# Attention and a greedy mixture of experts on one core: threshold searches in eight four-bit digits, and row lists from halves of 32 and 12 values

## The chip, the cores and the metric

The kernel runs on one core of one Trainium2 chip. A core has five engines that run their own instruction streams side by side: TensorE (PE, matrix products; its weight loads are listed apart as PEld), VectorE (DVE), ScalarE (ACT), GpSimd (POOL) and SyncE (SP, which issues most transfers here). They wait for one another by semaphores. The metric is the time of one execution on the device in microseconds, as the median of several runs; less is better.

## What is computed

First attention within clusters, then a layer of experts in which tokens are dealt out greedily by the size of their logits:

```python
N, D, E, F = (3072, 512, 8, 1024)
cap = N // E
logits = x @ w_gate            # x is the output of the attention
order = np.argsort(-logits.flatten())
for idx in order:
    tok, e = (int(idx) // E, int(idx) % E)
    if assigned[tok] >= 0 or counts[e] >= cap:
        continue
    assigned[tok] = e
    counts[e] += 1
...
for e in range(E):
    mask = assigned == e
    h = np.maximum(x[mask] @ w1[e], 0.0)
    out[mask] = h @ w2[e]
```

So each of the 8 experts gets exactly 384 of the 3072 tokens.

## The kernel before

Attention takes the first 370 us or so of the execution; the change touches none of its steps. The expert stage that follows treats the experts one after another, in the order in which they fill up. The code counts them p = 0 to 7; "the first expert" is p = 0, and "expert 2" means p = 2. For every expert there is

- a search for the logit at which it is full, digit by digit from the top. For each digit, `ind` (DVE) marks for 24 tokens a partition and each of the digit's values which tokens lie above it; `cnt` (PE, line 1212) counts the marks per expert; `blk0` and `blk1` (DVE) gather the counts; `pick` (PE, line 1240) spreads them over the partitions; `sat` (DVE) compares with 384; `dig` (PE, line 1253) turns the result into the threshold so far, which the next `ind` reads. After the upper digits `v` (DVE) forms the rest, and the next `ind` marks that.
- a row list of 384 token numbers. `top` and a few DVE steps (c1, c2, c3, ei, mq, gt, ge) name the expert; `rank` (PE, lines 1304 and 1305) ranks its members; `upe`, `scan`, `addr`, `stt0`, `pm`, `ph`, `pl` (DVE) turn ranks into a row number in two halves; `ohl` and `ohh` (DVE, lines 1341 and 1350) are one-hot marks of the low and of the high half; `ohv` (line 1344) is ohl times the token's number; `col` (PE, line 1357) multiplies ohv by ohh; `pb0`, `pb1` (DVE), `rep` (PE), `pi` and `idx` (DVE) put the list in place. Small tables of both stages lie in PSUM (`pk`, `pc`).
- `gx`, a gather of the 384 rows of x through the list (POOL's queue), and `xp` with `xc`, or `xt`, which bring them into place as `xgt`.
- eight weight loads (`w_load`, SP's queue), each issued once `reg` knows the expert's number, and their split in a high and a low 16-bit part: `wsc` and `whi` on ACT, `wlo` on POOL.
- `hid` (PE, line 1447): 8 blocks of 12 matmuls with 384 columns; after each block `rel` (ACT, writes hh) and `hlo` (DVE, line 1479, writes the rest hl). The products lie in five PSUM buffers `pf`.
- `out` (PE, line 1485): 72 matmuls with 512 columns, `oev` (ACT), and `sc`, the scatter to the output.

The order of the steps on each engine is fixed: a table written out in the source, `FFN_ORDER`, names the steps one after another, and each engine runs its own in that order. The search for expert p begins among the out matmuls of expert p-2 and ends, with the row list, among the hid matmuls of expert p-1. A step such as `cnt,3,1` is the count of digit 1 of expert 3; `hid,2,4,1,0` is a matmul of expert 2's block 4; `hlo,2,4` is the hl step of that block.

A search before has seven digits, of 5, 5, 5, 5, 4, 4 and 4 bits, 32 bits in all. For a 32-value digit `ind` works on 128x768, and the count is six matmuls of 32 columns; for a 16-value digit it is 128x384 and three matmuls of 64 columns. A row number of 0 to 383 is split in a low half of 16 and a high half of 24 values.

Of the kernel before, what the change touches and what calls it, by code (L numbers as in the profile page):

```python
# [191 lines left out]
w_load,0,1 stt0,0 pm,0 w_load,0,2 ph,0 pl,0 w_load,0,3 ohl,0 ohvp,0 ohh,0 lt,0 upd,0 col,0 wm,36 b,1,0 wm,37 wm,38 pb0,0
pb1,0 b,1,5 rep,0 wm,39 wm,40 b,1,6 wm,41 pi,0 wm,42 wm,43 idx,0 whi,0,0,B wm,44 wm,45 b,1,8 wm,46 gx,0,0 wm,47 b,1,1
wm,48 wm,49 wm,50 b,1,2 wm,51 wm,52 wm,53 wsc,0,1 wm,54 b,1,3 wm,55 wm,56 gx,0,1 b,1,4 b,1,9 whi,0,1,C gx,0,2 b,1,10
cnt,1,0,- wlo,0,0,B blk0,1,0 blk1,1,0 xph,0 xph,1 pick,1,0 xch,0 sat,1,0 xch,1 wsc,0,2 whi,0,2,C wsc,0,3 hid0,0,0,0,0
hid0,0,0,0,1 dig,1,0 ind,1,1,- hid0,0,4,0,0 hid0,0,4,0,1 wlo,0,1,C ei2 hid0,0,0,0,2 hid0,0,1,0,0 reg2 hid0,0,1,0,1
# [5 lines left out]
hid0,0,0,2,1 hid0,0,4,1,2 cnt,1,2,- hid0,0,5,1,0 hid0,0,5,1,1 hid0,0,5,1,2 hid0,0,6,1,0 blk0,1,2 hid0,0,6,1,1
hid0,0,6,1,2 hid0,0,7,1,0 hid0,0,7,1,1 blk1,1,2 hid0,0,7,1,2 hid0,0,4,2,0 hid0,0,4,2,1 hid0,1,0,0,0 wlo,0,3,C pick,1,2
hid0,0,0,2,2 hid0,0,1,2,0 hid0,0,1,2,1 sat,1,2 hid0,0,1,2,2 hid0,0,2,2,0 hid0,0,2,2,1 hid0,0,2,2,2 hid0,0,3,2,0 dig,1,2
hid0,0,3,2,1 hid0,0,3,2,2 hid0,0,0,3,0 hid0,0,0,3,1 v,1 hid0,0,4,2,2 hid0,0,5,2,0 hid0,0,5,2,1 hid0,0,5,2,2 ind,1,3,-
hid0,0,6,2,0 hid0,0,6,2,1 hid0,0,6,2,2 hid0,0,7,2,0 hid0,0,7,2,1 wsc,0,4 hid0,0,7,2,2 hid0,0,4,3,0 hid0,0,4,3,1
hid0,1,0,0,1 hid0,1,4,0,0 hid0,1,4,0,1 hid0,1,0,0,2 hid0,1,1,0,0 hid0,1,1,0,1 hid0,1,1,0,2 hid0,1,2,0,0 hid0,1,2,0,1
cnt,1,3,- hid0,0,0,3,2 hid0,0,1,3,0 hid0,0,1,3,1 whi,0,4,C hid0,0,1,3,2 blk0,1,3 hid0,0,2,3,0 hid0,0,2,3,1 hid0,0,2,3,2
hid0,0,3,3,0 blk1,1,3 hid0,0,3,3,1 hid0,0,3,3,2 hid0,0,4,3,2 hid0,0,5,3,0 pick,1,3 hid0,0,5,3,1 hid0,0,5,3,2
hid0,0,6,3,0 hid0,0,6,3,1 sat,1,3 hid0,0,6,3,2 hid0,0,7,3,0 hid0,0,7,3,1 wsc,0,5 hid0,0,7,3,2 wlo,0,4,C dig,1,3  # L210
hid0,1,2,0,2 hid0,1,3,0,0 hid0,1,3,0,1 hid0,1,3,0,2 ind,1,4,- hid0,1,0,1,0 hid0,1,0,1,1 hid0,1,4,0,2 hid0,1,5,0,0
hid0,1,5,0,1 hid0,1,5,0,2 hid0,1,6,0,0 hid0,1,6,0,1 hid0,1,6,0,2 cnt,1,4,- whi,0,5,C hid0,1,7,0,0 hid0,1,7,0,1
hid0,1,7,0,2 hid0,1,4,1,0 blk0,1,4 hid0,1,4,1,1 hid0,1,0,1,2 hid0,1,1,1,0 hid0,1,1,1,1 hid0,1,1,1,2 blk1,1,4
hid0,1,2,1,0 hid0,1,2,1,1 hid0,1,2,1,2 hid0,1,3,1,0 pick,1,4 hid0,1,3,1,1 hid0,1,3,1,2 wsc,0,6 hid0,1,0,2,0 hid0,1,0,2,1
wlo,0,5,C sat,1,4 hid0,1,4,1,2 hid0,1,5,1,0 hid0,1,5,1,1 hid0,1,5,1,2 dig,1,4 hid0,1,6,1,0 hid0,1,6,1,1 hid0,1,6,1,2
hid0,1,7,1,0 ind,1,5,- hid0,1,7,1,1 hid0,1,7,1,2 hid0,1,4,2,0 hid0,1,4,2,1 hid0,1,0,2,2 hid0,1,1,2,0 rel0,0,0
# [5 lines left out]
hid0,1,5,3,1 hid0,1,5,3,2 hid0,1,6,3,0 hid0,1,6,3,1 ind,1,6,- hid0,2,4,0,0 hid0,2,4,0,1 hid0,1,6,3,2 hid0,1,7,3,0
hid0,1,7,3,1 hid0,1,7,3,2 hid0,2,0,0,2 hid0,2,1,0,0 whi,0,7,C cnt,1,6,- hid0,2,1,0,1 hid0,2,1,0,2 hid0,2,2,0,0
hid0,2,2,0,1 blk0,1,6 hid0,2,2,0,2 hid0,2,3,0,0 hid0,2,3,0,1 hid0,2,3,0,2 hid0,2,0,1,0 blk1,1,6 hid0,2,0,1,1
hid0,2,4,0,2 hid0,2,5,0,0 hid0,2,5,0,1 pick,1,6 rel0,1,0 hid0,2,5,0,2 hid0,2,6,0,0 wlo,0,7,C hid0,2,6,0,1 hid0,2,6,0,2
sat,1,6 hid0,2,7,0,0 hid0,2,7,0,1 hid0,2,7,0,2 hid0,2,4,1,0 dig,1,6 rel0,1,1 top,1 hid0,2,4,1,1 hlo0,1,0,D hid0,2,0,1,2
# [10 lines left out]
lt,1 col,1 w_load,1,6 upd,1 hid0,2,7,3,2 out,0,0,3,0 pb0,1 rel0,2,1 out,0,0,3,1 w_load,1,7 out,0,0,3,2 pb1,1 out,0,0,4,0
out,0,0,4,1 wsc,1,0 b,2,0 rep,1 out,0,0,4,2 pi,1 out,0,0,5,0 idx,1 out,0,0,5,1 b,2,5 out,0,0,5,2 gx,1,0 b,2,6 whi,1,0,C
out,0,0,6,0 b,2,8 out,0,0,6,1 out,0,0,6,2 b,2,9 out,0,0,7,0 out,0,0,7,1 wsc,1,1 gx,1,1 out,0,0,7,2 out,0,1,0,0 b,2,1
out,0,1,0,1 out,0,1,0,2 b,2,2 out,0,1,1,0 whi,1,1,C out,0,1,1,1 b,2,3 gx,1,2 out,0,1,1,2 out,0,1,2,0 b,2,4 out,0,1,2,1  # L240
hlo0,1,1,D cnt,2,0,- wsc,1,2 out,0,1,2,2 wlo,1,0,C out,0,1,3,0 b,2,10 out,0,1,3,1 blk0,2,0 out,0,1,3,2 blk1,2,0
# [1297 lines left out]
```

## Time and profile before

| what | value |
|---|---|
| median of 3 runs (lowest to highest) | 676.03 us (675.4 to 678.72) |
| the profiled execution, its own time | 675.39 us |
| its span, from the first to the last instruction | 673.6 us |
| PE busy, share of the span | 644.6 us, 96% |
| DVE busy | 505.7 us, 75% |
| ACT busy | 418.9 us, 62% |
| POOL busy | 484.4 us, 72% |

The span is what the trace shows; the time of the execution is 1.8 us longer. Busy time is the sum of an engine's instructions without the gaps, and it mixes stages with different limits. Matmuls are pipelined: the duration of one in a row is longer than the distance to the next, and it is the distance that counts. A row of the trace in order of time has the start, the duration, the engine, the line, the operation, the tiles (out<-in), the shapes, and in brackets the idle time ahead of it with what ended it, where there was any.

### The profile page before, as it was taken

To read this page: it belongs to the slowest core of one execution; us is meant where nothing else is said; L and a number is where in the kernel's file an instruction comes from. 1 tells how busy PE (TensorE), PEld (TensorE's weight loads), DVE (VectorE), ACT (ScalarE), POOL (GpSimd) and SP (SyncE) were. 2 spreads that over 40 slices of the span, in tenths; PEclk is the share of its full clock that TensorE was granted. 3 is DMA by queue.
4 is the path that set the end of the run, shared out by engine and by line. 5 is a ranking of instruction groups with operands and counts; after the bars stand their busy time and mean duration, and the time that the engine had idled before them with its cause. 6 is when DMAs were issued, how large, how long until landed. Compare 5 with 4: busy or idle time off the path is not lost. (4 is left out here: it accounts for less than half of the span.)

```text
span 673.6 us, 19685 instructions
## 1 busy us (share of the span) xinstructions
PE 644.6 (96%) x8246; PEld 433.5 (64%) x8246; DVE 505.7 (75%) x1160; ACT 418.9 (62%) x552; POOL 484.4 (72%) x390
## 2 busy tenths in 40 slices
...
GB/s 191 197 205 167 163 153 231 114 179 164 169 197 132 168 178 139 98 142 55 52 50 74 26 175 130 307 92 300 150 241 208 183 251 157 264 322 164 48 1 47
DMA packets 175450, 105.84 MB, mean 157 GB/s; under 512 B 135426, under 2 KB 160002, under 8 KB 175362
## 3 DMA queue, kind: packets, MB, share of 16 engines
...
## 5 line engine op out<-in xcount | busy, mean ns | idle before, releaser
L838 POOL TENSOR_TENSOR rt<-pt 128x768 f16<-128x768 f32 x176 | 266.9, 1542 | 62.4 <-ACT pt L830 62.2
L830 ACT ACTIVATE pt<-sc 128x768 f32<-128x768 f32 x192 | 150.5, 811 | 102.3 <-PE sc L827 99.5
L788 DVE TENSOR_REDUCE mxs<-sc 128x1 f32<-128x768 f32 x192 | 178.7, 951 | 12.6 <-PE sc L784 11.2
L1447 PE MATMUL pf<-xgt,w1h 128*128 128x384 f16 (+1 forms) x640 | 129.6, 295 | 0.3 <-DVE xgt L1436 0.3
L860 PE MATMUL av<-vh,pt 128*128 128x66 f16 x1152 | 121.7, 194 | 0.2 <-DVE xb L893 0.2
L841 PE MATMUL av<-vh,rt 128*128 128x66 f16 x1152 | 121.4, 193 | 0.0
L862 PE MATMUL av<-vl,pt 128*128 128x64 f16 x1152 | 121.4, 191 | 0.0
L860 PEld LDWEIGHTS <-pt 128*128 128x128 bf16 x1152 | 106.0, 97 | 8.3
L862 PEld LDWEIGHTS <-pt 128*128 128x128 bf16 x1152 | 105.5, 98 | 8.7 <-issue 0.7
L841 PEld LDWEIGHTS <-rt 128*128 128x128 f16 x1152 | 104.7, 97 | 0.0
L823 PE MATMUL sc<-qbt,kbt 99*128 99x384 f16 x384 | 93.8, 325 | 1.0 <-DMA qbt<-mt 0.4
L827 PE MATMUL sc<-qat,kat 128*128 128x384 f16 x384 | 93.7, 325 | 0.0
L784 PE MATMUL sc<-kbt,qbt 80*128 80x384 f16 x384 | 90.2, 325 | 1.5 <-ACT qbt L746 0.7
L1447 PE MATMUL pf<-xgt,w1l 128*128 128x384 f16 (+1 forms) x320 | 90.5, 295 | 0.0
L1447 PEld LDWEIGHTS <-w1h 128*128 128x128 f16 x640 | 57.8, 98 | 28.5 <-issue 1.0
L1411 POOL TENSOR_TENSOR w2l<-wr,w2h 128x1024 f16<-128x1024 f32 x32 | 67.6, 2134 | 4.2 <-ACT w2h L1404 3.9
L1485 PE MATMUL pf<-w2h,hh 128*128 128x512 f16 x184 | 69.6, 378 | 0.0
L1485 PE MATMUL pf<-w2h,hl 128*128 128x512 f16 x184 | 69.4, 378 | 0.0
L1485 PE MATMUL pf<-w2l,hh 128*128 128x512 f16 x184 | 69.4, 378 | 0.0
L1401 ACT ACTIVATE wr<-wr 128x1024 f32<-128x1024 f32 x63 | 65.7, 1046 | 4.3 <-DMA wr<-in_moe_w_dram 3.6
L1411 POOL TENSOR_TENSOR w1l<-wr,w1h 128x1024 f16<-128x1024 f32 x31 | 65.4, 2136 | 0.3
L1479 DVE SCALAR_TENSOR_TENSOR hl<-pf,hh 128x384 f16<-128x384 f32 x56 | 30.7, 551 | 40.7 <-ACT hh L1476 36.6
(259 smaller groups left out, 1137.1 us busy)
## 6 DMA issues: line engine op xcount, KB each, us to landing
...
xg<-xrow,idx POOLq DMA_INDIRECT x24, 6.5
```

The costliest lines, as they stand in the source:

```text
L784: nc.tensor.matmul(p[:, half, :S // 2], QBT[u][:D + C, i, :], KBT[u][:D + C, h * J + half * 3:h * J + half * 3 + 3, :], start=True, stop=True)
L788: nc.vector.tensor_reduce(mxs[u % 3][:, i:i + 1], MP.pop((u, i))[:, :, :S // 2], axis=AX.XY, op=OP.max)
L823: nc.tensor.matmul(ps[:, half, :S // 2], KBT[u][:ER + 3, s, :], QBT[u][:ER + 3, cs, :], start=True, stop=False)
L827: nc.tensor.matmul(ps[:, half, :S // 2], KAT[u][:, s, :], QAT[u][:, cs, :], start=False, stop=True)
L830: nc.scalar.activation(pts[(u * 12 + s // 2) % RP][:, s % 2], MP.pop((u, "b", s))[:, :, :S // 2], AF.Exp, scale=ESC)
L838: (nc.vector if e == "D" else nc.gpsimd).tensor_sub(rts[x][:, s % 2], p.rearrange("p a b -> p (a b)"), hi_view(pts[x])[:, s % 2])
L841: nc.tensor.matmul(o[:, j, :], r[:, j * P:(j + 1) * P], VH[u][:, s, :], start=False, stop=(s % J == J - 1), skip_group_check=True)
L860: nc.tensor.matmul(o[:, j, :], hi[:, js], VH[u][:, s, :], start=(kt == 0 and j == 0), stop=False, skip_group_check=True)
L862: nc.tensor.matmul(o[:, j, :D], hi[:, js], VL[u][:, s, :], start=False, stop=False, skip_group_check=True)
L1411: nc.gpsimd.tensor_sub(lo, wrs[c], hi)
L1447: nc.tensor.matmul(o, (w1l if i == 2 else w1h)[x][:, c, fs], xgt[x][:, h + int(i == 1), ts], start=(first and i == 0), stop=(last and i == ...
L1485: nc.tensor.matmul(PS["o", p, g], (hl if i == 2 else hh)[x][:, f, g * P:(g + 1) * P], (w2l if i == 1 else w2h)[x][:, f, :], start=(f == 0 ...
```

## The change

From p = 2 on a search has eight digits of four bits: every `ind` is 128x384 and every count three matmuls of 64 columns. The tables for it (`offs4`, and `wdb4`, one for the upper and one for the lower four digits) are made on POOL with steps `tab4` and `wdb4`, put in behind `wdb` in the search of the first expert and behind the last `wlo` of that expert. `clr` clears the accumulators at the start of a search. From p = 1 on the row list takes a low half of 32 and a high half of 12 values: `ohl` and `ohv` go from 128x384 to 128x768, `ohh` from 128x576 to 128x288, `col` from three matmuls of 192 columns to six of 48, and `pb0`, `pb1`, `rep` and `pi` shrink.

```diff
+    SH4 = [28, 24, 20, 16, 12, 8, 4, 0]
+    offs4 = [rt.tile([P, 16], F32, name=f"offs4{r}") for r in range(4)] + [o[:, :16] for o in offs[3:]]
+    wdb4 = [rt.tile([P, P], BF16, name=f"wdb4{r}") for r in range(2)]
...
+    def lw(p):
+        return 32 if p else 16
...
+    def four(p):
+        return p >= 2
+
+    def digits(p):
+        return [16] * 8 if four(p) else DIG
...
     def f_cnt(p, r, h):
-        n, ind, oh = DIG[r], marks(p, r), ohs[w3(p)]
+        n, ind, oh = digits(p)[r], marks(p, r), ohs[w3(p)]
...
+    def f_wdb4(x):
+        nc.gpsimd.memset(wdb4[x], 0.0)
+        for i in range(4):
+            nc.gpsimd.memset(wdb4[x][32 * i:32 * i + 16, :], float(1 << SH4[4 * x + i]))
+            nc.gpsimd.memset(wdb4[x][32 * i:32 * i + 1, :], LEAST if i + x == 0 else 0.0)
+
+    def f_clr(p):
+        V.memset(satb, 0.0)
...
     def f_ohl(p):
-        V.tensor_tensor(ohl, plo[:, :, None].to_broadcast([P, NT, 16]), loc[:, None, :].to_broadcast([P, NT, 16]), op=OP.is_equal)
+        w = lw(p)
+        V.tensor_tensor(lo_of(ohl_, p), plo[:, :, None].to_broadcast([P, NT, w]),
+                        (loc32 if p else loc)[:, None, :].to_broadcast([P, NT, w]), op=OP.is_equal)
...
     def f_col(p):
-        k = GC[16]
-        PS["i"] = pq = pct.tile([P, k, CAP // 16], F32, name="pc")
+        k, w = GC[lw(p)], CAP // lw(p)
+        PS["i"] = pq = pct.tile([P, k, w], F32, name="pc")
         for i in range(0, NT, k):
-            nc.tensor.matmul(pq, ohv[:, i:i + k, :].rearrange("p t n -> p (t n)"), ohh[:, i:i + k, :],
+            nc.tensor.matmul(pq, lo_of(ohv_, p)[:, i:i + k, :].rearrange("p t n -> p (t n)"), hi_of(p)[:, i:i + k, :],
                              start=(i == 0), stop=(i + k == NT))
```

`FFN_ORDER` is written anew from the first count of expert 2 on; one line of it shows how:

```diff
-out,0,1,4,0 whi,1,2,C hlo0,2,0,D pick,2,0 out,0,1,4,1 out,0,1,4,2 out,0,1,5,0 sat,2,0 out,0,1,5,1 hlo0,2,1,D wsc,1,3
+out,0,1,3,0 b,2,10 out,0,1,3,1 out,0,1,3,2 pick,2,0 out,0,1,4,0 sat,2,0 whi,1,2,C hlo0,2,0,D out,0,1,4,1 out,0,1,4,2
```

Counted in PE work, the searches of experts 3 to 6 end 1.9, 2.7, 3.2 and 3.6 us later against the matmuls of the expert at hand, and the row lists, the first weight loads and the gathers of those experts with them. wsc, whi and wlo keep their places among the matmuls.

The first place is the row list of expert 5 on DVE. In the order before, the steps from upe (line 1328) to pb0 (line 1361) stand so; L1341 is ohl, L1350 ohh, L1344 ohv, L1325 lt and L1479 an hl step of expert 4:

```order
L1328 SCALAR_TENSOR_TENSOR L_98<-pk_8055,L_98 128x192
L1308 SCALAR_TENSOR_TENSOR tot_8083<-pc_10462,mk_8081 128x48
L1311 TENSOR_TENSOR pk_8055<-tot_8083,pc_10462 128x48
L1315 SCALAR_TENSOR_TENSOR pk_8055<-pk_8055,mk_8081 128x48
L1318 TENSOR_REDUCE pk_8055<-pk_8055 128x24
L1335 TENSOR_SCALAR pk_8055<-pk_8055 128x24
L1338 TENSOR_SCALAR pk_8055<-pk_8055 128x24
L1341 TENSOR_TENSOR ohl_8084<-pk_8055,loc_171 128x384
L1350 TENSOR_TENSOR ohh_8086<-pk_8055,hic_172 128x576
L1344 TENSOR_TENSOR ohv_8085<-ohl_8084,pk_8055 128x384
L1325 TENSOR_SCALAR pk_8055<-pk_8055 128x24
L1479 SCALAR_TENSOR_TENSOR hl0_8120<-pf_10404,hh0_8118 128x384
```

In the changed order the same stretch reads so; the line numbers are those of the changed source, in which L1546 is hl, L1402 ohl, L1413 ohh and L1406 ohv, and the fence begins with the first hl step behind upe:

```order
L1546 SCALAR_TENSOR_TENSOR hl0_8128<-pf_10437,hh0_8126 128x384
L1368 SCALAR_TENSOR_TENSOR tot_8091<-pc_10534,mk_8089 128x48
L1371 TENSOR_TENSOR pk_8055<-tot_8091,pc_10534 128x48
L1375 SCALAR_TENSOR_TENSOR pk_8055<-pk_8055,mk_8089 128x48
L1378 TENSOR_REDUCE pk_8055<-pk_8055 128x24
L1395 TENSOR_SCALAR pk_8055<-pk_8055 128x24
L1398 TENSOR_SCALAR pk_8055<-pk_8055 128x24
L1402 TENSOR_TENSOR ohl_8092<-pk_8055,loc32_8083 128x768
L1546 SCALAR_TENSOR_TENSOR hl0_8128<-pf_10461,hh0_8126 128x384
L1413 TENSOR_TENSOR ohh_8094<-pk_8055,hic32_8084 128x288
L1546 SCALAR_TENSOR_TENSOR hl0_8128<-pf_10487,hh0_8126 128x384
L1406 TENSOR_TENSOR ohv_8093<-ohl_8092,pk_8055 128x768
```

Three hl steps stand between upe and ohv where there was none; on PE, 22 hid matmuls lie between rank and col in both orders.

The second place is PE in the round of expert 3 in which v is formed. Before, between the dig (line 1253) and the first of the six matmuls of the next count (line 1212), there are seven out matmuls (the rows of the weight loads ahead of each matmul are left out here and in the next piece):

```order
L1253 MATMUL pc_9554<-satb_8067,wdb2_8071 128x1
L1485 MATMUL pf_9541<-w2h1_8109,hl1_8121 128x512
L1485 MATMUL pf_9541<-w2h1_8109,hh1_8119 128x512
L1485 MATMUL pf_9541<-w2l1_8111,hh1_8119 128x512
L1485 MATMUL pf_9541<-w2h1_8109,hl1_8121 128x512
L1485 MATMUL pf_9541<-w2h1_8109,hh1_8119 128x512
L1485 MATMUL pf_9541<-w2l1_8111,hh1_8119 128x512
L1485 MATMUL pf_9541<-w2h1_8109,hl1_8121 128x512
L1212 MATMUL pc_9568<-oh2_8059,ind1_8061 128x32
```

After (dig is line 1313, out line 1552, the count line 1249):

```order
L1313 MATMUL pc_9605<-satb_8067,wdb40_8081 128x1
L1552 MATMUL pf_9579<-w2h1_8117,hl1_8129 128x512
L1552 MATMUL pf_9579<-w2h1_8117,hh1_8127 128x512
L1552 MATMUL pf_9579<-w2l1_8119,hh1_8127 128x512
L1552 MATMUL pf_9579<-w2h1_8117,hl1_8129 128x512
L1249 MATMUL pc_9614<-oh2_8059,ind1_8061 128x64
```

Four out matmuls are left between the two, and the `ind` between them on DVE has 128x384 in place of 128x768.

The third place is DVE in expert 3's first round. Before, the hl steps (line 1479) of expert 1 stand around blk0 (1217), blk1 (1220), sat (1246) and ind (1193) so:

```order
L1479 SCALAR_TENSOR_TENSOR hl1_8121<-pf_9329,hh1_8119 128x384
L1217 TENSOR_TENSOR cq_8062<-pc_9458,own32_179 128x32
L1220 TENSOR_REDUCE cs_8063<-cq_8062 128x8
L1479 SCALAR_TENSOR_TENSOR hl1_8121<-pf_9365,hh1_8119 128x384
L1246 TENSOR_SCALAR scr0_8064,satb_8067<-pc_9475 32x8
L1479 SCALAR_TENSOR_TENSOR hl1_8121<-pf_9388,hh1_8119 128x384
L1193 SCALAR_TENSOR_TENSOR ind1_8061<-pk_8055,pc_9483,offs1_156 128x768
```

After, with hl at line 1546, clr at 1295, sat at 1305 and ind at 1230:

```order
L1546 SCALAR_TENSOR_TENSOR hl1_8129<-pf_9365,hh1_8127 128x384
L1295 MEMSET satb_8067 128x1
L1255 TENSOR_TENSOR cq_8062<-pc_9501,own16_177 128x64
L1258 TENSOR_REDUCE cs_8063<-cq_8062 128x8
L1546 SCALAR_TENSOR_TENSOR hl1_8129<-pf_9401,hh1_8127 128x384
L1305 TENSOR_SCALAR scr0_8064,satb_8067<-pc_9510 16x8
L1230 SCALAR_TENSOR_TENSOR ind1_8061<-pk_8055,pc_9518,offs41_8078 128x384
L1546 SCALAR_TENSOR_TENSOR hl1_8129<-pf_9424,hh1_8127 128x384
```

The last hl step of expert 1, which the third out matmul behind dig reads, now stands behind ind, and before it stood ahead of it.

## Rows read from the trace of the kernel before

**Rows 1.** Busy time by stretch: span, then us, busy (instructions) of each engine, clock, DMA.

```profile
core 0 of [0], span 673.6 us
...
500.00:550.00 50.00, 50.00 (x342) 26.62 (x341) 35.23 (x124) 28.93 (x39) 33.26 (x21) 1.00 0.57 177
```

**Rows 2.** PE in order of time, search of expert 3: counts, digs and neighbours.

```profile
491.32 0.30 PE L1212 MATMUL pc<-oh,ind 128*128 128x32 bf16 x6
491.48 0.38 PE L1485 MATMUL pf<-w2h,hh 128*128 128x512 f16 x1
...
499.46 0.17 PE L1253 MATMUL pc<-satb,wdb 128*128 128x1 bf16 x1
...
501.00 0.32 PE L1212 MATMUL pc<-oh,ind 128*128 128x32 bf16 x6
...
503.62 0.26 PE L1212 MATMUL pc<-oh,ind 128*128 128x64 bf16 x3
503.71 0.38 PE L1485 MATMUL pf<-w2h,hl 128*128 128x512 f16 x1
...
505.25 0.17 PE L1253 MATMUL pc<-satb,wdb 128*128 128x1 bf16 x1
...
506.16 0.26 PE L1212 MATMUL pc<-oh,ind 128*128 128x64 bf16 x3
```

**Rows 3.** PE in order of time: rank and col of expert 2, col of expert 5.

```profile
450.78 0.19 PE L1304 MATMUL pc<-mk,tri 128*128 128x48 bf16 x1
...
454.40 0.41 PE L1357 MATMUL pc<-ohh,ohv 128*128 128x192 f16 x3
454.65 0.49 PE L1447 MATMUL pf<-xgt,w1h 128*128 128x384 f16 x2
...
547.37 0.41 PE L1357 MATMUL pc<-ohh,ohv 128*128 128x192 f16 x3
```

**Rows 4.** DVE in order of time: ohv of experts 2 and 5.

```profile
453.67 0.54 DVE L1344 TENSOR_TENSOR ohv<-ohl,pk 128x384 f16<-128x384 f16 x1
...
546.72 0.54 DVE L1344 TENSOR_TENSOR ohv<-ohl,pk 128x384 f16<-128x384 f16 x1
```

**Rows 5.** DVE by form, 400 to 640: count, busy us, mean ns, idle before.

```profile
L1193 DVE SCALAR_TENSOR_TENSOR ind<-pk,pc,offs 128x384 bf16<-128x384 f32 x18 | 11.2, 622 | 6.9 <-PE pc L1253 6.9
...
L1350 DVE TENSOR_TENSOR ohh<-pk,hic 128x576 f16<-128x576 int32 x7 | 5.2, 747 | 0.0
...
L1341 DVE TENSOR_TENSOR ohl<-pk,loc 128x384 f16<-128x384 int32 x7 | 3.9, 557 | 0.2
```

**Rows 6.** DVE in order of time: an hl step of expert 2, v of expert 3.

```profile
485.49 0.54 DVE L1479 SCALAR_TENSOR_TENSOR hl<-pf,hh 128x384 f16<-128x384 f32 x1
485.96 0.17 DVE L1371 SCALAR_TENSOR_TENSOR pg<-pc,own 128x24 f32<-128x24 f32 x1
...
499.70 0.26 DVE L1197 SCALAR_TENSOR_TENSOR pk<-pk,pc,lop 128x24 f32<-128x24 int32 x1 [0.50 <-issue]
499.99 0.96 DVE L1191 TENSOR_TENSOR ind<-pk,offs 128x768 bf16<-128x768 f32 x1
```

**Rows 7.** PE in order of time: searches of expert 2 (two rows) and expert 3.

```profile
437.35 0.38 PE L1485 MATMUL pf<-w2h,hl 128*128 128x512 f16 x1
437.75 0.16 PE L1253 MATMUL pc<-satb,wdb 128*128 128x1 bf16 x1
...
473.35 0.17 PE L1240 MATMUL pc<-cs,rep 128*128 128x8 f16 x1 [0.40 <-DVE cs L1220]
```

**Rows 8.** DVE in order of time: copies into xgt in expert 2's search.

```profile
436.20 1.29 DVE L748 COPY xgt<-pf 128x1024 f16<-128x1024 f16 x2 [0.45 <-PE pc L1240]
```

**Rows 9.** POOL in order of time: the first expert's search and list.

```profile
391.78 0.83 POOL L1347 TENSOR_TENSOR ohv<-ohl,vals 128x384 f16<-128x384 f16 x1 [6.58 <-DVE ohl L1341]
```

**Rows 10.** SP's queue in order of time: first weight loads of expert 6.

```profile
576.53 2.12 SPq L1387 DMA_DIRECT2D wr<-in_moe_w_dram  x4
```

**Rows 11.** ACT in order of time: expert 6's first wsc.

```profile
580.21 1.06 ACT L1401 ACTIVATE wr<-wr 128x1024 f32<-128x1024 f32 x1 [0.71 <-DMA wr<-in_moe_w_dram]
```

More of the change, by code (lines that the diff above doesn't have):

```diff
@@ L192 @@
[L192 to L196, printed above, removed]
@@ L202 @@
[L202 to L206, printed above, removed]
@@ L207 @@
[L207 to L216, printed above, removed]
@@ L222 @@
[L222 to L226, printed above, removed]
@@ L237 @@
[L237 to L241, printed above, removed]
@@ L257 @@
[L257 to L259 removed]
+sat,0,1 wdb,5 dig,0,1 ind,0,2,0 ind,0,2,1 cnt,0,2,0 wdb,6 cnt,0,2,1 sat,0,2 dig,0,2 wdb,7 tab4,0 tab4,1 tab4,2 tab4,3
+tab4,4 tab4,5 wdb4,0 v,0 ind,0,3,0 ind,0,3,1 cnt,0,3,0 cnt,0,3,1 sat,0,3 dig,0,3 ind,0,4,0 ind,0,4,1 cnt,0,4,0 cnt,0,4,1
@@ new lines @@
+sat,0,4 dig,0,4 ind,0,5,0 ind,0,5,1 cnt,0,5,0 cnt,0,5,1 sat,0,5 dig,0,5 ind,0,6,0 ind,0,6,1 cnt,0,6,0 cnt,0,6,1 sat,0,6
+dig,0,6 top,0 c1,0 c2,0 c3,0 ei,0 mq,0 reg,0 gt,0 ge,0 es2,0 rank,0 wm,0 upe,0 wm,29 wm,30 w_load,0,0 wm,31 scan,0 wm,32
+wm,33 wm,34 addr,0 wm,35 w_load,0,1 stt0,0 pm,0 w_load,0,2 ph,0 pl,0 w_load,0,3 ohl,0 ohvp,0 ohh,0 lt,0 upd,0 col,0
+wm,36 b,1,0 wm,37 wm,38 pb0,0 pb1,0 b,1,5 rep,0 wm,39 wm,40 b,1,6 wm,41 pi,0 wm,42 wm,43 idx,0 whi,0,0,B wm,44 wm,45
+b,1,8 wm,46 gx,0,0 wm,47 b,1,1 wm,48 wm,49 wm,50 b,1,2 wm,51 wm,52 wm,53 wsc,0,1 wm,54 b,1,3 wm,55 wm,56 gx,0,1 b,1,4
@@ L281 @@
-blk1,3,6 hid,2,2,0,0 wlo,2,7,C hid,2,2,0,1 rel,2,1 pick,3,6 hid,2,2,0,2 hid,2,2,1,0 sat,3,6 hid,2,2,1,1 hlo,2,1 dig,3,6
-top,3 hid,2,2,1,2 hid,2,2,2,0 hid,2,2,2,1 c1,3 hid,2,2,2,2 c2,3 hid,2,2,3,0 hid,2,2,3,1 c3,3 hid,2,2,3,2 ei,3
-hid,2,3,0,0 mq,3 reg,3 hid,2,3,0,1 rel,2,2 hid,2,3,0,2 gt,3 hid,2,3,1,0 ge,3 hid,2,3,1,1 es2,3 rank,3 hid,2,3,1,2 upe,3
-hid,2,3,2,0 w_load,3,0 hid,2,3,2,1 scan,3 hid,2,3,2,2 hid,2,3,3,0 addr,3 hid,2,3,3,1 w_load,3,1 hid,2,3,3,2 stt0,3
-hid,2,4,0,0 pm,3 hid,2,4,0,1 rel,2,3 w_load,3,2 hid,2,4,0,2 ph,3 hid,2,4,1,0 pl,3 hid,2,4,1,1 ohl,3 hid,2,4,1,2
@@ L306 @@
-wlo,3,7,C hid,3,0,1,0 sat,4,5 hid,3,0,1,1 dig,4,5 hid,3,0,1,2 hid,3,0,2,0 ind,4,6,- hid,3,0,2,1 hid,3,0,2,2 hid,3,0,3,0
-cnt,4,6,- hid,3,0,3,1 hid,3,0,3,2 blk0,4,6 hid,3,1,0,0 blk1,4,6 hid,3,1,0,1 rel,3,0 hid,3,1,0,2 sc,2,2 pick,4,6
-hid,3,1,1,0 hid,3,1,1,1 sat,4,6 hid,3,1,1,2 hlo,3,0 dig,4,6 top,4 hid,3,1,2,0 hid,3,1,2,1 hid,3,1,2,2 c1,4 hid,3,1,3,0
-c2,4 hid,3,1,3,1 hid,3,1,3,2 c3,4 hid,3,2,0,0 ei,4 hid,3,2,0,1 rel,3,1 mq,4 reg,4 hid,3,2,0,2 hid,3,2,1,0 gt,4
-hid,3,2,1,1 ge,4 hid,3,2,1,2 es2,4 rank,4 hid,3,2,2,0 upe,4 hid,3,2,2,1 w_load,4,0 hid,3,2,2,2 scan,4 hid,3,2,3,0
@@ new lines @@
+hid,2,7,3,2 out,2,0,0,0 b,4,9 wlo,3,0,C out,2,0,0,1 out,2,0,0,2 out,2,0,1,0 gx,3,2 rel,2,7 out,2,0,1,1 b,4,1 out,2,0,1,2
+wsc,3,2 hlo,2,5 out,2,0,2,0 out,2,0,2,1 out,2,0,2,2 b,4,2 out,2,0,3,0 wlo,3,1,C whi,3,2,C out,2,0,3,1 b,4,3 hlo,2,6
+out,2,0,3,2 out,2,0,4,0 b,4,4 out,2,0,4,1 hlo,2,7 out,2,0,4,2 b,4,10 clr,4 cnt,4,0,- blk0,4,0 blk1,4,0 wsc,3,3
+out,2,0,5,0 out,2,0,5,1 out,2,0,5,2 out,2,0,6,0 pick,4,0 sat,4,0 out,2,0,6,1 wlo,3,2,C whi,3,3,C out,2,0,6,2 out,2,0,7,0
+dig,4,0 ind,4,1,- out,2,0,7,1 out,2,0,7,2 wsc,3,4 out,2,1,0,0 out,2,1,0,1 cnt,4,1,- blk0,4,1 blk1,4,1 out,2,1,0,2
```

514 lines of the change are left out of this document (290 added, 224 removed).

## The prediction, made before the change was run

> **What bounds the kernel now.** The first view is the table of busy time by stretch. Attention fills the first 370 us and no instruction of it is touched, so only the expert stage after it can move. There TensorE (PE) is busy 50.00 of 50 us at a granted clock of 1.00 while VectorE (DVE) has 35.23, in a span of 673.6 us [rows 1]. In such a stage only two things change the time: PE instructions taken out or put in, and moments in which PE, whose program order is fixed, comes to an instruction whose input isn't there. The second view, PE's instructions in order of time, is read for the distance between two instructions that a chain on DVE connects. The third, DVE's instructions in order of time, gives the length of that chain. A stall is length minus distance. DVE's share of busy time says nothing about it: DVE waits for PE most of a digit round, and yet is on the path from one PE instruction of a round to the next.
>
> How tight the distances are: in the row list of expert 2, rank is issued at 450.78 and col at 454.40, so 3.62 us later, with 22 hid matmuls between (0.162 us each) [rows 3]. The last DVE step that col needs, ohv, runs from 453.67 for 0.54 and ends at 454.21 [rows 4]: 0.19 before col. In expert 5 it is 546.72 + 0.54 = 547.26 against a col at 547.37, 0.11 [rows 3, 4]. Part of that is the hand-off from DVE to PE, which is at most 0.11; so the slack is 0 to 0.11 in expert 5 and 0.08 to 0.19 in expert 2. I take 0.05 on average over the lists. The order leaves these lists no room.
>
> **The change part by part.**
>
> *PE work.* A count of six 32-column matmuls takes 491.48 - 491.32 = 0.16 of PE's time, one of three 64-column ones 503.71 - 503.62 = 0.09 [rows 2]. A search had four of the first and three of the second, 0.91; it gets eight of the second, 0.72, and one more pick and dig at 0.03 each (499.46 for a dig, of which seven out matmuls at 0.215 leave 0.03 up to 501.00 [rows 2]): -0.13, in five searches -0.65. A col of three 192-column matmuls takes 454.65 - 454.40 = 0.25 [rows 3]; six of 48 columns lie between six of 32 (0.16) and three of 192 twice over (0.50). They are nearest to the first, 0.17: -0.08 for seven lists, -0.55. PE work: **-1.2** (bounds: -1.3 with col at 0.16, +1.1 with col at 0.50). That six small matmuls, each with a load of its own, cost 0.16, so 27 ns each, is what the price of col rests on [rows 2].
> The Trainium skill, TensorE: Matmul & The Clock Gate, section Back-to-back issue gap, gives a stream of weight load and matmul about 81 ns for each matmul at 128 columns, and speaks against the list part: three matmuls more in each of seven lists would be an estimated +1.7, seven fewer in each of five searches -2.8, together -1.1. Its table for single matmuls has a floor near 25 ns up to 64 columns, by which counts and col together would give -1.6. The trace, with 27 ns, goes with the floor.
>
> *The list chain gets longer.* ohl and ohv go from 384 to 768 elements a partition, ohh from 576 to 288. ohl takes 557 ns at 384 and ohh 747 at 576 [rows 5]: 0.99 ns an element. So ohl + 0.38, ohv + 0.38 (0.54 at 384, [rows 4]), ohh - 0.28: **+0.48 to +0.51** on the path from rank to col; below, a slope of half on the wide 16-bit ohv would leave +0.2, above there is nothing to add. I take 0.51. The distance on PE stays at 22 hid matmuls for experts 2 to 6, by the order of both programs, so nothing hides it but 0.05 of slack. Expert 1's list is in the same position. The seventh list has its col many out matmuls later and waits for nothing. Six lists at 0.46: +2.8.
>
> *hl steps move into that chain.* The new order puts hl steps (hlo) between rank and ohv on DVE: one in expert 3, two in expert 4, three each in expert 5 and expert 6; before, none, as the DVE rows of expert 5 in the order show. hl runs 0.54, and the next step begins 0.47 after it (485.49 to 485.96 [rows 6]). They read PSUM tiles that ScalarE (ACT) has long served, so they run at once, and each delays col by 0.47: nine of them, **+4.2**. Less only if hl fell in a hole of DVE; there is one, the wait for rank's result ahead of scan, which upe already fills. Together the lists cost 2.8 + 4.2 = **+7.0**: about 0.5 in experts 1 and 2, 0.9, 1.4, 1.9 and 1.9 in experts 3 to 6. What is late next: pb0, rep and the gathers of the same list, and after the stall DVE has caught up.
>
> *Digit rounds.* A 16-value round needs 0.91 from dig to the next count (505.25 to 506.16 [rows 2]), made of 0.24 to the first DVE step (499.46 to 499.70), ind's 0.62 and the hand-off 0.05 [rows 2, 5, 6]. The new order leaves 0.84 to 1.10: little lost. Three rounds are worse:
> the round after v has 0.24 + 0.29 (v, 499.70 to 499.99) + 0.56 (ind at 384, by ohl's form) + 0.05 = 1.14 to run, where the order now puts four out matmuls, 0.89 with dig, in experts 3 and 6 and five, 1.10, in 4 and 5 (before: seven, 1.54, for a 768-wide ind): +0.6 in all [rows 2, 5, 6];
> in expert 3's first round an hl step that the next out matmul reads stands behind ind: 0.24 + 0.62 + 0.47 + 0.05 = 1.38 against 0.46 of PE work (dig and two out matmuls), +0.9, while the stall before that expert's pick at 473.35, 0.40 by the row [rows 7], goes away: +0.5;
> in expert 2, two copies of 1.29 together [rows 8] now stand between the count and sat of one round: 0.8 for blk0 and blk1, 1.3, and 0.23 to dig make 2.3, against about 1.4 of PE work (the count, one group of transposes, four out matmuls); and a third copy of 0.6 ahead of v makes the next count need 1.5 against 0.89: +1.5. The 0.8 is an estimate: of the 1.63 from the count at 503.62 to the dig at 505.25 three out matmuls and a pick are 0.67, and hand-offs some 0.15 [rows 2]. So +1.5, less what the copies cost there now (the out matmul ahead of dig begins at 437.35 and takes 0.215, so dig at 437.75 stands 0.18 late [rows 7], and I take as much for the count after it): +1.1.
> Rounds that were 0.03 to 0.08 short before are longer now: -0.3. Rounds: **+1.9** (bounds +0.5, if copies start early and hl is quick, and +3).
>
> *What is hidden.* The tables for four-bit digits, fifteen small steps on GpSimd (POOL) in the first expert's search, go into its idle stretch of 6.58 us ahead of 391.78 [rows 9]; at some 0.25 each (they follow one another like the memsets ahead of it) they need 3.7. If that cover were gone, 1 to 3 us in a stage where PE waits anyway. The second table lies in a later hole. clr, a memset on DVE for each search, stands where DVE waits.
>
> *Weights.* An expert's weight loads are issued once its search is done: for expert 6 at 576.53, its first wsc on ACT begins at 580.21 [rows 10, 11], 3.7 later. Searches of experts 3 to 6 end 2 to 3.6 us later in PE's work, while wsc stays where it was. So ACT will hold up to 3 us in front of a rel there; five PSUM buffers stand between that rel and PE. I give it 0, with up to +4.
>
> **The sum.** -1.2 + 7.0 + 1.9 = +7.7. The profiled execution has 675.39 us of its own, a span of 673.6 and 1.8 around it; 683.1. The median of before, 676.03, lies 0.6 above its profiled run, so the median forecast is **683.5** to 683.7, 1.1% slower.
>
> **The rivals.**
> Only the list gets longer, and the hl steps are free, because they run in holes: +7.7 - 4.2 = +3.5, 679.5. Against it: the list's DVE rows follow one another without a gap [rows 5]. 0.13.
> Weights late: ACT's hold reaches PE in one or two of the experts, +4 on top, 687.5. For it: 0.6 us of PE work where 3.7 is needed; against it, the buffers. 0.13.
> The other side, no slower: DVE steps that follow one another overlap more than I count. Already the step behind an hl begins 0.47 after it where hl lasts 0.54 [rows 6]. If wide steps and hl steps between rank and ohv overlap with their neighbours so far that an hl adds under 0.1 and the wider steps nothing, rank to ohv stays at its length and the 7.0 go: -1.2 + 1.9 = +0.7, so 676.1 and a median of 676.7; with the rounds at their lower bound of 0.5, 675.3. Against it: an overlap of 0.07 is what the row of hl shows [rows 6], and ind at 768 took 0.96 [rows 6], as 0.99 an element gives from 0.557. 0.10.
> The chance for the forecast is 0.64. Its own range: lists 5.5 to 7.5, rounds 0.5 to 3, PE work -1.5 to -0.65: 680.5 to 686. With the neighbours on both sides, 678 to 688. Faster by over 0.5% (which is about what can be told from no change here) 0.05, within it 0.13, slower 0.82.
>
> **What would show it.** In the profile after: col's idle time ahead of it, released by DVE's ohv, in experts 2 to 6, growing from 0.4 to 1.9; ohl and ohv near 0.95, ohh near 0.46; six col matmuls in under 0.2 us; PE busy under 48 of 50 us in the stretches from 450 on; a stall of 0.2 at the count after v. It is wrong if col follows its hid matmuls without a gap, or if PE's main stall stands at a hid or xt instruction, waiting for weights.

## The result, and the profile after

The changed kernel took 685.33 us as a median of four runs (684.28 to 686.06), the kernel before 675.96 (four runs, 675.4 to 678.72): a ratio of 1.0126 with a 95% interval of 1.0107 to 1.0145. The forecast was 683.5, slower, within 678 to 688. One of the twelve executions of best16 below took 1089.73 us at a mean granted clock of 0.557 and is left out of its figures.

The profiled execution has a span of 683.9 us, 10.3 more than before. Not all of that belongs to the change. The busy time by stretch of the attention stage, whose instructions are the same in both programs, shows it; after PE's busy time come PEld, DVE, ACT and POOL, then the granted clock. First the changed kernel:

```profile
165.00:175.00 10.00, 9.38 (x137) 6.47 (x137) 7.82 (x17) 4.13 (x6) 6.10 (x5) 0.66 1.01 160
...
170.00:172.00 2.00, 2.00 (x22) 1.32 (x19) 1.89 (x3) 0.00 (x0) 2.00 (x2) 0.50 2.01 195
```

And the same stretch in the kernel before:

```profile
165.00:175.00 10.00, 9.35 (x197) 7.47 (x196) 9.68 (x20) 5.60 (x9) 8.13 (x7) 1.00 0.97 160
```

In this one execution the clock fell to 0.50, 1.2 GHz, for some microseconds, and PE issued 137 matmuls there in place of 197. DVE's steps start within 0.05 us of those before from 100 to 166 us and 2.8 us later from 175 us on, and so does rank of the first expert (391.94, before 389.13). Such a dip stands in six of the twelve profiles of this document, at instructions that are the same in all of them, so it most likely comes and goes between executions; each kernel was profiled once, so this isn't shown for one kernel. Attention differs between profiles elsewhere too: lists16 below, without a dip, is 2.6 us behind at the same place.

The place to compare is therefore the stage itself, from the start of expert 1's rank to the end of the span. That rank before and after:

```profile
419.51 0.19 PE L1304 MATMUL pc<-mk,tri 128*128 128x48 bf16 x1
```

```profile
422.35 0.19 PE L1364 MATMUL pc<-mk,tri 128*128 128x48 bf16 x1
```

So the stage has 673.6 - 419.5 = 254.1 us before and 683.9 - 422.4 = 261.5 after. **The change costs 7.4 us there.** The sum of the forecast for that stage was +7.7. From the first expert's rank to expert 1's, a stretch with the wait for the first expert's gather, the profiles have 29.3 to 31.6 us, so that expert 1's rank is the first place from which they can be compared to some tenths of a microsecond.

Busy time by stretch in the expert stage of the changed kernel, which answers to [rows 1]:

```profile
450.00:500.00 50.00, 48.07 (x319) 25.28 (x317) 36.30 (x133) 31.46 (x41) 31.09 (x21) 1.00 0.63 213
500.00:550.00 50.00, 48.85 (x326) 25.24 (x324) 31.23 (x117) 31.38 (x40) 39.16 (x23) 1.00 0.63 177
550.00:600.00 50.00, 46.57 (x313) 25.21 (x312) 35.41 (x127) 29.95 (x41) 27.63 (x19) 1.00 0.62 210
```

The first of these stretches before, of which the second is in [rows 1]:

```profile
450.00:500.00 50.00, 49.60 (x333) 26.07 (x332) 37.13 (x127) 36.20 (x45) 35.35 (x23) 1.00 0.82 246
```

PE, which had 49.60 and 50.00 of 50 us there, and 50.00 in the third, now waits 1.2 to 3.4 us in each stretch, at the full clock. What it waited for is the next view, the groups of PE's waits from 380 to 650 (total, number, longest):

```profile
PE pc L1421 <- DVE ohv L1406: 5.6, 6, 1.7
...
PE pf L1552 <- DVE hl L1546: 0.8, 1, 0.8
PE pc L1313 <- DVE scr L1305: 0.6, 1, 0.6
...
PE pc L1249 <- DVE ind L1228: 0.4, 1, 0.4
```

The first is col of six row lists. The rows left out behind it belong to the first expert's search, list and gather, ahead of the stage compared here, and those left out further down have 0.5 us or less each. PE in order of time at the cols of experts 1 to 6 (the page's idle time begins at the modelled end of the matmul ahead, about 0.16 after its successor could have been issued):

```profile
426.32 0.32 PE L1421 MATMUL pc<-ohh,ohv 128*128 128x48 f16 x6 [0.30 <-DVE ohv L1406]
...
458.92 0.32 PE L1421 MATMUL pc<-ohh,ohv 128*128 128x48 f16 x6 [0.21 <-DVE ohv L1406]
...
491.90 0.32 PE L1421 MATMUL pc<-ohh,ohv 128*128 128x48 f16 x6 [0.83 <-DVE ohv L1406]
...
524.96 0.32 PE L1421 MATMUL pc<-ohh,ohv 128*128 128x48 f16 x6 [0.98 <-DVE ohv L1406]
...
559.12 0.32 PE L1421 MATMUL pc<-ohh,ohv 128*128 128x48 f16 x6 [1.69 <-DVE ohv L1406]
559.28 0.32 PE L1514 MATMUL pf<-xgt,w1l 128*128 128x384 f16 x1
...
593.81 0.32 PE L1421 MATMUL pc<-ohh,ohv 128*128 128x48 f16 x6 [1.55 <-DVE ohv L1406]
```

Six matmuls take 559.28 - 559.12 = 0.16, where three took 0.25 [rows 3]. Reckoned from start to start the cols stand 0.47, 0.38, 0.99, 1.15, 1.85 and 1.72 us late: 6.6 in all. Why expert 5's is 1.85 late is seen on DVE, in order of time from upe to ohv, against [rows 4]:

```profile
553.73 0.36 DVE L1388 SCALAR_TENSOR_TENSOR L<-pk,L 128x192 f32<-128x192 f32 x1
554.01 0.55 DVE L1546 SCALAR_TENSOR_TENSOR hl<-pf,hh 128x384 f16<-128x384 f32 x1
554.47 0.25 DVE L1368 TENSOR_TENSOR_SCAN tot<-pc,mk 128x48 f32<-128x48 f32 x1
...
555.95 0.96 DVE L1402 TENSOR_TENSOR ohl<-pk,loc 128x768 f16<-128x768 int32 x1
556.83 0.55 DVE L1546 SCALAR_TENSOR_TENSOR hl<-pf,hh 128x384 f16<-128x384 f32 x1
557.29 0.45 DVE L1413 TENSOR_TENSOR ohh<-pk,hic 128x288 f16<-128x288 int32 x1
557.65 0.55 DVE L1546 SCALAR_TENSOR_TENSOR hl<-pf,hh 128x384 f16<-128x384 f32 x1
558.12 0.94 DVE L1406 TENSOR_TENSOR ohv<-ohl,pk 128x768 f16<-128x768 f16 x1
```

Nothing on DVE waits: from upe to ohv's end step follows step, and each of the three hl steps takes 0.46 to 0.47 of the chain. ohv ends at 559.06 and col starts at 559.12. The forms on DVE, against [rows 5]:

```profile
L1402 DVE TENSOR_TENSOR ohl<-pk,loc 128x768 f16<-128x768 int32 x7 | 6.7, 956 | 0.2
L1406 DVE TENSOR_TENSOR ohv<-ohl,pk 128x768 f16<-128x768 f16 x7 | 6.6, 943 | 0.0
...
L1413 DVE TENSOR_TENSOR ohh<-pk,hic 128x288 f16<-128x288 int32 x7 | 3.1, 447 | 0.0
```

956, 943 and 447 ns. The digit rounds of experts 2 and 3 on PE (dig and count of expert 2's v round, then the out matmul that waits for expert 1's last hl, then expert 3's v round):

```profile
441.95 0.16 PE L1313 MATMUL pc<-satb,wdb 128*128 128x1 bf16 x1 [0.58 <-DVE scr L1305]
...
443.43 0.26 PE L1249 MATMUL pc<-oh,ind 128*128 128x64 bf16 x3 [0.43 <-DVE ind L1228]
...
467.84 0.60 PE L1552 MATMUL pf<-w2h,hl 128*128 128x512 f16 x2 [0.76 <-DVE hl L1546]
...
475.68 0.38 PE L1552 MATMUL pf<-w2h,hl 128*128 128x512 f16 x1
476.15 0.26 PE L1249 MATMUL pc<-oh,ind 128*128 128x64 bf16 x3
```

Reckoned from start to start they are 0.74, 0.59, 0.92 and, from 475.68 + 0.215 to 476.15, 0.25 us late.

### The profile page after: what moved, and what is told of

Read it like the earlier page. It is cut to its first block, busy times and chain, and to the rows that moved or that the text cites. A ratio compares the mean times of both kernels' runs of the same rounds, so it can differ in the third digit from the quotient of the medians.

```text
span 683.9 us, 19714 instructions
## 1 busy us (share of the span) xinstructions
PE 647.1 (95%) x8232; PEld 433.3 (63%) x8232; DVE 506.7 (74%) x1190; ACT 418.1 (61%) x552; POOL 489.4 (72%) x414
## 4 chain that ended last, share of the span: by engine, by line
PE 74%; DVE 11%; ACT 4%; issue 2%; DMA 2%; POOLq 0%; POOL 0%; DVEq 0%; ACTq 0%
PE pf L1552 16%; PE pf L1514 13%; PE sc L827 8%; PE sc L831 8%; PE sc L788 8%; PE av L864 5%; PE av L845 5%; PE av L866 4%; PE mx L671 2%; ACT pt L834 1%; DVE hl L1546 1%; DVE ohl L1402 1%; PE pc L1249 1%; DVE mxs L792 1%; PE av L870 1%
## 5 line engine op out<-in xcount | busy, mean ns | idle before, releaser
L1482 POOL DMA_INDIRECT xg<-xrow,idx x24 | 24.0, 998 | 58.1 <-DVE pk L1050 16.8
```

## The experiments

The theory to be tested is the forecast's: PE's 22 hid matmuls between rank and col are a fixed distance, and whatever lengthens DVE's chain from rank to ohv stalls PE by the excess; hl steps in it cost most. The rival is that the later weight loads, for which ACT waits 15.6 us between 420 and 640 in the changed kernel (0.7 before), are the real cost. In this table the stage is the span's end less the start of expert 1's rank, from one profile each. The ratio is against the kernel before of the same session, whose medians were 675.96 for the changed kernel, 677.26 for hl_out to digits4, 677.42 for wsc_late to best32 and 676.84 for the last two; it is an estimate of its own and not exactly the quotient of the two medians. An expectation in absolute time such as lists32's starts from the 676.0 of the first session, 1.3 us under the median it is then held against.

| kernel | median us | ratio, 95% interval | stage, over before (us) |
|---|---|---|---|
| changed kernel | 685.33 | 1.0126 (1.0107 to 1.0145) | 261.5, +7.4 |
| hl_out | 681.51 | 1.0080 (1.0054 to 1.0105) | 258.3, +4.2 |
| lists16 | 684.27 | 1.0114 (1.0091 to 1.0137) | 260.8, +6.7 |
| lists32 | 677.72 | 1.0015 (0.9997 to 1.0034) | 255.6, +1.5 |
| digits4 | 681.24 | 1.0055 (1.0035 to 1.0075) | 260.3, +6.1 |
| wsc_late | 684.73 | 1.0127 (1.0098 to 1.0157) | 262.2, +8.1 |
| digits4_wsc | 680.85 | 1.0068 (1.0041 to 1.0096) | 258.6, +4.5 |
| best16 | 679.91 | 1.0038 (1.0017 to 1.0059) | 257.1, +3.0 |
| best32 | 678.62 | 1.0024 (1.0005 to 1.0043) | 255.6, +1.5 |
| lists32_col | 676.13 | 0.9988 (0.9967 to 1.0008) | 253.3, -0.8 |
| best32_rel | 676.64 | 1.0005 (0.9985 to 1.0025) | 253.8, -0.3 |

In the cuts of the order below, "..." stands for steps left out, and a bare hid or out for one matmul of that kind.

**hl_out.** The hl steps leave the list's chain; for expert 6, for instance:

```diff
-rank,6 hlo,5,0 ... ohl,6 hlo,5,1 ... ohh,6 hlo,5,2 ... ohv,6 hlo,5,3 lt,6 col,6
+ind,6,7,- hlo,5,0 ... rank,6 ... ohl,6 ... ohh,6 ... ohv,6 lt,6 col,6 hlo,5,1 ... pb1,6 hlo,5,2 ... idx,6 hlo,5,3
```

> The changed kernel, with the hl steps that stand between rank and ohv on DVE put elsewhere: behind col or pb1 of the list, the first ones of experts 4 and 5 into the last digit round. Theory (the list's DVE chain against 22 hid matmuls): col's stalls fall from 1.0, 1.15, 1.85 and 1.7 us in experts 3 to 6 to about 0.45 each, 4 us less, some 0.3 of it given back at rep or a count: 681.5 us. Rival (the later weight loads and what ACT holds are the cost, and a stall taken away at col comes back at a later hid or out): 684.5 to 685.5.

681.5, and in the trace col's lateness fell from 6.6 to 2.9 us, with 0.35 to 0.53 in experts 2 to 6, as expected. In experts 3 to 6, whose hl steps were moved, it fell by 3.9; expert 1's col, whose order is the same, stood 0.74 late instead of 0.47. PE's waits at col in this kernel:

```profile
PE pc L1420 <- DVE ohv L1405: 1.9, 6, 0.6
```

Of the 3.7 us the stage gained 3.2: 0.6 came back at expert 6's first count. The hl steps were the larger part of the loss, and the rival falls for the changed kernel: ACT waits as long for weights here as there (15.0 us from 420 to 640, 15.6 in the changed kernel), and the stalls went all the same.

**lists16.** One line gives every list the old halves:

```diff
     def lw(p):
-        return 32 if p else 16
+        return 16
```

> The changed kernel with its order, but row lists of 16 by 24 as before: ohl and ohv at 384, ohh at 576, col three matmuls of 192 columns. Theory: each of six chains is 0.5 shorter, col's stalls 0, 0, 0.5, 0.65, 1.35 and 1.2 us, 2.8 less in all, and col itself 0.08 dearer in seven lists: 683.0 us. Rival (the time per element of a wide one-hot step isn't on the path): 685.5 to 686.

684.3 where 683.0 was expected. At col it went as the theory has it: experts 1 and 2 wait no more, the others 0.49, 0.64, 1.35 and 1.21 us, 2.9 less in all. But the stage gained only 0.7. What took it back stands in PE's waits of this kernel:

```profile
PE pc L1421 <- DVE ohv L1406: 3.0, 4, 1.2
PE pc L1434 <- DVE cs L1430: 0.8, 2, 0.5
...
PE pc L1249 <- DVE oh L1058: 0.7, 1, 0.7
```

rep (L1434) waits for the wider pb0 and pb1, 0.9 more than in the changed kernel, expert 6's first count for a DVE step of its own search, 0.6 more, and seven cols cost 0.09 more each. The expectation had missed the first two. The medians alone don't tell this kernel from the changed one (their intervals overlap); the 0.7 rests on one trace of each.

**lists32.** The order and the seven digits of before, with the lists of 32 by 12:

```diff
     def four(p):
-        return p >= 2
+        return False
```

> The kernel before with its order and its seven digits, and only the row lists of 32 by 12. Theory: six lists stall 0.4 to 0.5 each at col, 2.7 us, col is 0.08 cheaper seven times and the short waits at rep go: 678.0 us, slower by 2.0. Rival (the whole loss comes from the new order, the lists are free or a gain of 0.6): 675.4.

677.7 against 677.3, in the trace +1.5. The six cols are late by 0.37 to 0.47, 2.6 in all, and PE waits for little else:

```profile
PE pc L1417 <- DVE ohv L1402: 1.6, 6, 0.3
PE pc L1295 <- DVE cs L1254: 0.4, 1, 0.4
```

Six stalls of 2.6, less 0.6 for seven cheaper cols and 0.5 of waits at rep that went, make the 1.5. The theory's terms hold, but its total of 2.0 had left out the waits at rep in part; the median differs by 0.5 us, and the ratio's interval, -0.2 to 2.3 us, holds the 1.5.

**digits4.** lists16 and hl_out together.

> The changed kernel with lists of 16 by 24 and the hl steps out of the list's chain: eight four-bit digits and their order remain. Theory: col waits for nothing, and what is left over the kernel before are the digit rounds, +1.9, less 0.7 of PE work for the counts: 677.0 to 678.0 us. Rival (later weights): 681 or more. Second rival (the digit rounds are free): 675.0.

681.2, 3 to 4 us over the theory, and what the rival said. col waits for nothing. But ACT, DVE and PE near the end of expert 4 read so (a wsc, the last rel, the hl behind it, and expert 6's first count), with the clock of two stretches below:

```profile
555.22 1.06 ACT L1467 ACTIVATE wr<-wr 128x1024 f32<-128x1024 f32 x1 [3.08 <-DMA wr<-in_moe_w_dram]
...
562.33 0.47 ACT L1542 ACTIVATE hh<-pf 128x384 f16<-128x384 f32 x1
...
562.84 0.56 DVE L1545 SCALAR_TENSOR_TENSOR hl<-pf,hh 128x384 f16<-128x384 f32 x1 [1.79 <-ACT w1h L1470]
...
564.51 0.25 PE L1248 MATMUL pc<-oh,ind 128*128 128x64 bf16 x3 [2.21 <-DVE oh L1057]
...
562.00:564.00 2.00, 0.30 (x2) 0.02 (x1) 1.13 (x3) 1.97 (x4) 1.98 (x2) 1.00 1.04 398
...
566.00:568.00 2.00, 2.00 (x8) 0.73 (x7) 0.66 (x3) 1.82 (x2) 2.00 (x2) 0.50 0.85 168
```

ACT is held 3.08 us at the first wsc, whose weights were issued only when the longer search was done; from then on it works off wsc and whi with the rel steps between them, the last rel is late, the last hl waits for it, and the next search's DVE steps stand behind that hl. (The page puts the wait of that hl down to the whi ahead of the rel; the hl starts 0.04 after the rel's end.) PE waits 2.2 us, and behind its wait it runs at 0.50, 1.2 GHz, for some 3 us.

In the changed kernel the same hold was hidden. Reckoned from start to start, expert 6's first count is 0.26 us late there, 0.83 in hl_out and in lists16, and 2.37 here, while the stalls at the cols of the stage come to 6.6, 2.9, 3.7 and 0 us: over these four traces, the less PE loses at col, the more of the hold it meets at that count. How much of it a usual execution meets is less sure. The profiled one took 683.44 us, among the slowest of twelve (678.01 to 683.83), and its stage is 6.1 us over before, where the ratio gives 3.7 (2.4 to 5.1).

**wsc_late.** The changed kernel, with only this order altered on ACT (here for expert 5):

```diff
-wsc,5,0 ... whi,5,0,C ... rel,4,4 ... wsc,5,1
+rel,4,4 wsc,5,0 ... whi,5,0,C wsc,5,1
```

> The changed kernel, with only ACT's order altered: the first wsc and whi of experts 3 to 6 come one to three rel steps later, so that ACT no longer holds a rel while it waits for weights. Theory (in the changed kernel col's stalls give the weights their time, so what ACT holds costs PE at most the 0.3 us in front of expert 6's first count): 685.0 us, no change to the changed kernel. Rival (the hold costs PE more than that): 683 or less.

684.7, with a stage of +8.1: no gain. ACT's waits for weights from 420 to 640 fell by half; first the changed kernel's, then this one's:

```profile
ACT wr L1468 <- DMA wr<-in_moe_w_dram: 15.6, 6, 5.1
```

```profile
ACT wr L1468 <- DMA wr<-in_moe_w_dram: 7.9, 3, 6.2
```

col's stalls are the same to 0.01, and a new wait of 0.7 at expert 5's first count came. So what ACT holds was no part of the change's loss, but for at most the 0.26 at expert 6's first count, which is still there.

**digits4_wsc.** The same move in digits4.

> digits4 with the first wsc and whi of experts 3 to 6 later on ACT in the same way. In digits4's trace PE waited 2.4 us at expert 6's first count, behind an hl that waited for a rel that ACT held behind a wsc whose weights weren't there, and the granted clock fell to 0.50 behind that wait. Theory (late weights): the wait and the slow stretch go, 4 us less: 677.3 us. Rival (the wait has another cause, the DVE steps of the next search): 680.5 to 681.

680.9, 3.5 over expected, and in the range of the rival. Against digits4 the stage of the one profile is 1.7 us shorter, but the ratios (1.0068 and 1.0055) show no gain. The dip of the clock in the expert stage is gone from this trace, 1.8 us of wait remain at expert 6's first count, and 0.7 came at expert 5's. Ahead of that first count ACT and DVE read so:

```profile
559.29 1.06 ACT L1471 ACTIVATE w1h<-wr 128x1024 f16<-128x1024 f32 x1
560.25 0.47 ACT L1543 ACTIVATE hh<-pf 128x384 f16<-128x384 f32 x1
...
560.76 0.56 DVE L1546 SCALAR_TENSOR_TENSOR hl<-pf,hh 128x384 f16<-128x384 f32 x1 [1.85 <-ACT hh L1543]
```

It is still the hl that waits for the last rel, 1.85 us, and not DVE's own queue, as the rival had it. But the weights are hardly late any more (ACT waits 0.94 us for them at the first wsc of expert 5): wsc and whi, 1.06 us each, now stand in pairs ahead of the same rel. The late rel was named rightly, the late weights explain it only in part.

**best16.** digits4_wsc with the rounds mended:

```diff
-hlo,1,5 out clr,3 cnt,3,0,- blk0,3,0 blk1,3,0 ... pick,3,0 hlo,1,6 ... sat,3,0 ... dig,3,0 ind,3,1,- hlo,1,7
+hlo,1,5 hlo,1,6 out clr,3 cnt,3,0,- blk0,3,0 blk1,3,0 hlo,1,7 ... pick,3,0 ... sat,3,0 ... dig,3,0 ind,3,1,-
```

> digits4_wsc with the digit rounds mended: in expert 3 two hl steps go ahead of the first count and behind its blk1, in expert 2 two copies are moved, and the count after v comes one matmul later in experts 2, 3 and 6. Theory: 1.7 us of the rounds' stalls go, 675.5 us, as much as the kernel before or 0.3 less. Rival (mended rounds lose it elsewhere): 677.

679.9. The stage is 1.5 us shorter in the trace, of 1.7 expected: the 0.92 in expert 3 is gone, the count after v is 0.04 late in experts 3 and 6 and 0.25 in expert 2, where a hid matmul behind that count now waits 0.50 for ACT's oev. The base was 3.5 too high, so the median was too.

**best32.** As best16, with lists of 32 by 12 and col and what follows it three hid matmuls later.

> The changed kernel with its lists of 32 by 12, hl steps out of the chain, wsc later, the rounds mended as in best16, and col with the rest of the list three hid matmuls later. Theory: no stall at col, col 0.08 cheaper seven times: 0.5 under best16, 675.0 us. Rival (the list's later end delays gathers or hl steps): 677 or more.

678.6, and 1.5 us less than best16 in the trace, where 0.5 was expected; the base was again too high. col waits 0.04 at most. The waits left include 0.98 and 0.50 us at the first counts of experts 6 and 5, and 0.65 at a pick and 0.50 at a hid matmul in expert 2's search. The first two are one group of PE's waits:

```profile
PE pc L1249 <- DVE oh L1058: 1.1, 2, 0.8
```

**lists32_col.** lists32 with the same move of col:

```diff
-ohv,6 hid hid hid lt,6 col,6 ... pb0,6 ... pb1,6 ... rep,6 ... pi,6 ... idx,6 ... gx,6,0
+ohv,6 hid hid hid lt,6 hid hid hid col,6 ... pb0,6 ... pb1,6 ... rep,6 ... pi,6 ... idx,6 ... gx,6,0
```

> lists32 (the kernel before with lists of 32 by 12 and seven digits), with col, pb0, pb1, rep, pi, idx and the first gather three hid or out matmuls later in the order. Theory: the six stalls at col, 2.6 us in lists32's trace, go, and what is left of the list part is its gain: col's 0.08 seven times and 0.5 of waits at rep: in the trace 1.0 us less than the kernel before from expert 1's rank to the end, a median 0.5 to 1.5 under the kernel before's of the same session. Rival (a stall comes back at rep or at a gather): as the kernel before or slower.

676.1 against 676.8: in the trace -0.8, in the medians a ratio whose interval holds 1. No col and no rep stands in its list of PE's waits:

```profile
PE pc L1296 <- DVE cs L1255: 0.4, 1, 0.4
PE pc L1310 <- DVE scr L1302: 0.3, 1, 0.3
```

**best32_rel.** best32 with the rel of an expert's last block ahead of a wsc and a whi:

```diff
-wsc,5,2 ... whi,5,2,C ... rel,4,7 ... wsc,5,3
+rel,4,7 wsc,5,2 whi,5,2,C ... wsc,5,3
```

> best32 with the last rel step of experts 3 to 5 ahead of two wsc and whi steps on ACT. In best32's trace PE waited 0.5 and 1.0 us at the first counts of experts 5 and 6, behind an hl that waited for that rel. Theory: both waits go, 1.3 us less from expert 1's rank to the end, within 0.5 us of the kernel before. Rival (DVE's own queue holds that count): at most 0.3 less.

676.6 against 676.8. Both waits at the first counts are gone, 1.8 us of the stage with them; PE's waits from 420 to 640 are now

```profile
PE pc L1299 <- DVE cs L1258: 0.5, 1, 0.5
PE pf L1514 <- ACT ot L1570: 0.3, 1, 0.3
PE pf L1514 <- DVE hl L1546: 0.2, 1, 0.2
```

All parts of the change are in this kernel, and it costs what the kernel before costs (1.0005, 0.9985 to 1.0025). So the digits and the halves lose nothing once the order fits them; the loss was the order, with the old place of col for the longer lists as part of it (lists32). Nor do they gain what the forecast counts for PE work, 1.2 us: the stage has 0.3 less than before.

## Why the prediction was right

*The list chain.* Right, and by its mechanism. 7.0 was forecast for the six cols and 6.6 measured; by expert 0.5, 0.5, 0.9, 1.4, 1.9, 1.9 against 0.47, 0.38, 0.99, 1.15, 1.85, 1.72. The wider steps came out at 956, 943 and 447 ns for estimates of 0.95, 0.94 and 0.46. lists32 shows their part alone, 2.6 at col for the forecast's 2.8; hl_out the part of the hl steps, 3.9 in experts 3 to 6 for 4.2. (With half the slope on ohv the forecast's own terms give 0.3 for a list and not the 0.2 that it names as the lower bound; nothing hangs on it.) The over-estimate in the hl steps has this reason: one that stands between two steps that depend on each other can take less of the chain than 0.47. In expert 4 the hl ahead of ohl begins 0.10 behind the start of pl, where in the lists of before ohl itself began 0.22 behind it, so it added 0.35.

*Rounds.* +1.9 forecast. The three places were late by 0.74 and 0.59 (expert 2), 0.92 (expert 3) and 0.25 (after v, in experts 3 and 6; in 4 and 5 nothing). Reckoned from start to start over all rounds of the stage, PE was 3.84 us late in the changed kernel and 1.77 before: +2.1. The size is right, and in part by luck: 0.3 at expert 6's first count wasn't in the sum, while expert 2's two waits were 1.3, not 1.5, and the two after v 0.5, not 0.6. The stall ahead of expert 3's pick before, taken as 0.40 from the idle time in its row, is 0.56 from start to start.

*PE work.* 0.09 for a count, as priced from [rows 2], and 0.16 for a col, where 0.17 was priced.

*Weights.* At most 0.3 us in the changed kernel, where the sum had 0; wsc_late shows it. But the reason given, five PSUM buffers, is not what hid them. digits4 shows that the same hold costs 2 to 4 us once col's stalls are gone: the stalls hid it. As a rival it was priced well and its condition was wrong.

*The signs.* col, the widths, the six col matmuls and the count after v came as named, the count after v in experts 3 and 6 with 0.25 for 0.2. PE busy under 48 of 50 us came in one of the three stretches shown (46.57; 48.07 and 48.85 in the others).

*The sum.* -1.2 + 6.6 + 2.1 = +7.5 by the measured terms, +7.4 in the trace, +7.7 forecast. The median rose by 9.4 for the ratio's interval of +7.2 to +9.8; the profile puts 2.8 of its own 10.3 in attention, by the clock. How far that dip also weighs in the other three runs isn't shown, as only one execution was profiled.
